# Four zero-filling stores of a gated attention and Mish mix, issued behind the gate's transfers in place of the opening

## The chip, the cores and the metric

The kernel runs on one core of a Trainium2 chip. The metric is the device time of one execution in microseconds (us). The core has a matrix engine (PE, whose weight loads are listed as PEld), a vector engine (DVE), a scalar engine (ACT), a general engine (POOL) and a sync engine (SP), which here does nothing but issue DMAs. Each engine works through its own list of instructions in order, and they wait for one another by semaphores.

## The reference

One input `x` of 2048 rows and 640 columns in bf16 goes through two branches, which a gate mixes row by row:

```python
g = sigmoid((x * gate_w).sum(-1, keepdims=True))
a = attention(x, wqkv) @ wo      # 32 heads of 20 columns, softmax over 2048 keys
h = x @ w1 + b1                  # 1536 columns
b = (h * tanh(softplus(h))) @ w2
out = g * a + (1 - g) * b
```

## The kernel before

**Tiling.** The rows are cut into four blocks of 512 queries (`QC`, `NQC = 4`), the 32 heads into eight head groups of four (`NQ = 8`). A head has 20 columns, and four heads lie in 32 partitions each, with 12 partitions of padding. A group `G` of the attention is one head group `p` with one block of queries `qc`; there are 32 of them. The first five head groups run one after the other through all four blocks (so groups 0 to 3 belong to head group 0, groups 4 to 7 to head group 1), the last three block by block.

**What a group does.** PE makes score tiles of 128 keys by 512 queries (line 1073), four heads at a time from four partition ranges. ACT takes the exponential of most of them (line 1091), and DVE and POOL work out the exponential of the others by integer arithmetic (lines 586 and 616). PE adds up the products with the values (line 1108). `normalise` divides by the sums and stores the result into `o_dram` (line 1184).

**Projections.** They run between the scores, in pieces of five matrix products (line 663). Queries and keys of head groups 1 to 7, and the queries of head group 0 from the second block on, take a way through HBM: DVE copies a product into a staging tile `st` (line 752; three tiles in turn), SP stores it into `q_dram` or `k_dram` (line 755), and later SP loads it into the padded tiles `qT` (`load_q`, line 780, four DMAs, one a head) or `kT` (`load_k`, line 772, four DMAs). The keys of head group 0 are made in place; their product `first_k_chain` also yields the 48 last key columns in the 12 padding partitions of each head, which `store_top` sends to `k_dram` (line 719, four DMAs of 12 partitions by 512 columns for each of the four blocks).

**The order of the work.** After the opening everything is issued in an order written out by hand (`ORDER`), one letter a step: `S` and `D` are score products, `x` an exponential on ACT, `F` a piece of a projection, `y` a waiting DVE operation, `q` and `k` the loads of queries and keys, `e` the three steps of the gate. A DVE operation can have a follow-up, such as a store, that is issued with it. SP's queue holds its DMAs in the order in which these steps call them.

**The opening.** It loads `x` and the first weights and transposes blocks 2 and 3 of `x` by DMA (line 472). Then it issues on SP the strips of weights `ws` (line 432), the value weights `wv` (line 1234, 800 KB), and the four stores that the change touches (lines 1245 to 1250). The first steps of `ORDER` follow: on SP's queue these are the four times four DMAs of line 719, two stores of line 755 into `q_dram` between and behind them, and the load of the queries of group 1 (step `q1`).

**The zeros.** In the last block of queries the two last head groups (`NSB = 2`) never go to `o_dram`: they stay on the chip in the tiles `O`, are multiplied by the gate's rows `g_rows`, and meet the zero-padded rows of `wo` (`wo_pad`) in the last products. Their 160 columns of these 512 rows in `o_dram` would be empty, but the transposing loads of line 923 read whole column blocks at the end of the kernel. So four stores of 128 rows by 160 columns (40 KB each) put zeros there. Their source is `wo_pad[7]`, which POOL has set to zero (line 1244) at 8 to 9 us, and into which line 1277 loads weights at 345 us and later.

**The gate.** Step `e0` (`gate_values`) is an exponential on ACT, `e1` loads `wo`, and `e2` (`gate_rest`) finishes the gate on DVE (lines 1256 to 1258), writes the last block's values into `g_dram` in four DMAs (line 1262), and reads them back into all partitions as `g_rows` in four more (line 1267). `g_rows` is read at line 1146, twice, from 657 us on. In `ORDER` the steps run `e0`, `e2`, and `e1` much later.

Of the kernel before, what the change touches and what calls it, by code (L numbers as in the profile page):

```python
# [9 lines left out]
P = 128  # L10
# [298 lines left out]
def kernel(  # L309
# [12 lines left out]
    nc = tc.nc  # L322
    _, S, D = A_x.shape
# [6 lines left out]
    QC = 512  # L330
    NQC = S // QC
    NU = QC // P
    NQ = H // 4
# [12 lines left out]
    NSB = 2  # L346
# [49 lines left out]
    wo_pad = {}  # L396
# [11 lines left out]
    o_dram = dram.tile([S, D], BF16, tag="o_dram", name="o_dram")  # L408
# [15 lines left out]
    HF = 4 * DH  # L424
# [78 lines left out]
    for n in (1, 2, 4, 8, 16):  # L503
        nc.vector.tensor_scalar(
            out=count[:, n : 2 * n], in0=count[:, 0:n], scalar1=float(n), scalar2=None, op0=ALU.add
        )
    nc.vector.transpose(out=count[:, 32:64], in_=count[:, 0:32])
    for k in range(0, P, 32):
        nc.vector.tensor_tensor(
            out=ident[k : k + 32, k : k + 32], in0=count[k : k + 32, 0:32],  # L510
# [405 lines left out]
    LQ = NQC - 1  # L916
# [297 lines left out]
    def first_product(bank, w, cols):  # L1214
# [14 lines left out]
        out=wv0[:, :, 4 * DH : 4 * DH + 1], in_=gate_w.rearrange("(kt p o) -> p kt o", p=P, o=1)  # L1229
# [8 lines left out]
        out=wkp[:, :, :, DH:32], in_=w_top[:, :, :].rearrange("p k (h d) -> p k h d", h=4)  # L1238
# [3 lines left out]
        wo_pad[p] = consts.tile([P, D], BF16, tag=tag, name=f"wo{p}")  # L1242
    for t_ in (*wo_pad.values(), *qTb[1 : NQT - 1], *T2, *kTb[1:]):
        nc.gpsimd.memset(t_, 0.0)
    for u in range(NU):
        r0 = LQ * QC + u * P
        nc.sync.dma_start(
            out=o_dram[r0 : r0 + P, (NQ - NSB) * HF : D],
            in_=wo_pad[NQ - 1][:, 0 : D - (NQ - NSB) * HF],
        )  # L1250

    def gate_values():
        nc.scalar.activation(g_t[:, :], z_t[:, :], ACT.Exp, scale=-1.0)
# [1 line left out]
    def gate_rest():  # L1255
        nc.vector.tensor_scalar(out=g_t, in0=g_t, scalar1=1.0, scalar2=None, op0=ALU.add)
        nc.vector.reciprocal(out=g_t, in_=g_t)
        nc.vector.tensor_scalar(
            out=g1_t, in0=g_t, scalar1=-1.0, scalar2=1.0, op0=ALU.mult, op1=ALU.add
        )  # L1260
        for r in range(4):
            nc.sync.dma_start(
                out=g_dram[:, :].rearrange("i (b r) -> i b r", r=4)[:, :, r],
                in_=g_t[32 * r : 32 * r + 32, NU * LQ : NU * LQ + NU],
            )
        for k in range(4):
            nc.sync.dma_start(out=g_rows[32 * k : 32 * k + 32, :], in_=g_dram[:, :])

    def load_wo():
        wo_sb[0] = work.tile([P, KT, D], BF16, tag="wvwo", name="wo_sb")  # L1270
        nc.sync.dma_start(
            out=wo_sb[0][:, :, :], in_=A_wo.rearrange("(kt p) c -> p kt c", p=P)
        )
        for p in wo_pad:
            for k in range(4):
                r0 = (4 * p + k) * DH
                nc.sync.dma_start(
                    out=wo_pad[p][32 * k : 32 * k + DH, :], in_=A_wo[r0 : r0 + DH, :]
                )
# [11 lines left out]
    def begin(k, bank):  # L1291
# [6 lines left out]
        "o": lambda qc, a, b: load_o(qc, range(a, b)),  # L1298
        "v": make_vd,
        "e": lambda i: (gate_values, load_wo, gate_rest)[i](),  # L1300
        "l": load_late,
        "d": d_take,
# [94 lines left out]
```

## Time and profile before

| | |
|---|---|
| median of 3 runs | 685.68 us (684.23 to 686.0) |
| the profiled execution, time | 685.34 us |
| its span, first to last instruction | 683.6 us |
| granted TensorE clock | 1.00 |
| the four stores issued | from 21.3 us, the last at 24.1 us |
| the gate's stores (line 1262) and loads (line 1267) issued | from 66.1 us, and from 72.2 to 74.1 us |
| first transposing load that reads `o_dram` | 480.5 us |

A row of the timeline or of the chain of waits has the start in us, the length in us, the engine, the line, the operation, the tiles it writes and reads, the count of instructions that are merged in it, and, where the engine was idle before it, for how long and what ended that. `SPq` stands for SP's sequencer, and its rows are the issues of DMAs: the length is the time that SP spends on issuing, not that of the transfer. In a row of the waits stand the total in us, the count, and the longest. In a row of windows stand the window, its length, the busy time and count of instructions of each engine, then the clock, the DMA engines' busy share and GB/s. In a row of one tile the three durations are the shortest, the median and the longest in ns.

### The profile page before, as it was taken

Reading aid. Unit: us, or ns where it says so; the run is one execution under the profiler, and the core shown is the slowest. Engines: PE = TensorE matmul, PEld = TensorE weight load, DVE = VectorE, ACT = ScalarE, POOL = GpSimd, SP = SyncE. Lnnn points to the kernel's source line nnn. Section 1 sums busy time; section 2 is a strip of 40 time slices with the busy share of each in tenths; the row PEclk is TensorE's granted clock in tenths of the full one; section 3 lists DMA queues with packets and bytes.
Section 4 is the critical chain, followed back from the end, with each engine's and each line's share of the span. In section 5 each row is a group of like instructions: output and inputs, shape, how many; then the busy total and the mean of one; then the engine's idle time right before and its main releaser. Section 6 shows DMA issues by size and latency. Waiting matters only on the chain.

```text
span 683.6 us, 24516 instructions
## 1 busy us (share of the span) xinstructions
PE 672.5 (98%) x10355; PEld 234.2 (34%) x10355; DVE 597.4 (87%) x1033; ACT 667.1 (98%) x692; POOL 354.0 (52%) x349
## 2 busy tenths in 40 slices
PE   8989999999999999999999999999999999999997
PEld 4433232323323443323333222222243333333334
DVE  5679989898989989898878988999999988799896
ACT  6999999999999999999999999999999999999996
POOL 5135555545463635565555654456546654555453
PEclk9999999999999999999999999999999999999999
DMA  8444321312311211111241223321232111141221
GB/s 170 106 88 148 64 50 38 67 40 55 95 27 37 61 46 36 26 35 32 37 104 33 41 55 72 66 51 38 56 94 57 21 48 30 41 66 35 59 86 59
DMA packets 128542, 40.47 MB, mean 59 GB/s; under 512 B 94960, under 2 KB 127872, under 8 KB 128432
## 3 DMA queue, kind: packets, MB, share of 16 engines
q1 hardware_dynamic: 126032, 38.29, 25.7%
q8 instruction: 81, 1.33, 0.9%
q10 hardware_dynamic: 2400, 0.62, 0.4%
q14 instruction: 29, 0.24, 0.1%
HBM read 22.29 MB, written 12.78 MB: 51 GB/s over the span
## 4 chain that ended last, share of the span: by engine, by line
PE 87%; ACT 8%; DVE 2%; issue 1%; DMA 1%; SPq 1%; POOL 0%; ACTq 0%; DVEq 0%
PE Sp L1073 29%; PE Sp L1108 29%; PE Sp L663 28%; ACT E L1091 6%; ACT big L871 2%; DVE T L586 1%; DMA wf<-in_A_wqkv_dram 1%; SPq L719 0%; PE Sp L1336 0%; DMA qT<-q_dram 0%; DVE T L1151 0%; DVE ot L1353 0%; PE Sp L1217 0%; PE Sp L1123 0%; ACT L1091 0%
## 5 line engine op out<-in xcount | busy, mean ns | idle before, releaser
L1091 ACT ACTIVATE E<-Sp 128x1024 bf16<-128x1024 f32 (+2 forms) x674 | 634.8, 1126 | 6.0 <-PE Sp L1073 5.1
L616 POOL INT64_ADD T<-T x334 | 344.1, 1042 | 315.9 <-DVE T L586 210.3
L586 DVE TENSOR_SCALAR T<-Sp 128x512 int16<-128x512 f32 x668 | 440.4, 683 | 57.7 <-PE Sp L1073 47.3
L1073 PE MATMUL Sp<-qT,kT 32*128 32x512 bf16 x2048 | 259.8, 384 | 4.6 <-DMA qT<-q_dram 1.8
L1073 PEld LDWEIGHTS <-kT 32*128 32x128 bf16 x2048 | 70.2, 91 | 246.5 <-issue 241.7
L1108 PE MATMUL Sp<-E,VA 128*21 128x512 bf16 x1380 | 128.0, 382 | 0.0
L1108 PE MATMUL Sp<-T,VD 128*21 128x512 bf16 x1288 | 117.9, 382 | 0.1
L663 PE MATMUL Sp<-w_sb,big 128*32 128x320 bf16 x1536 | 72.9, 302 | 0.2 <-DVE T L586 0.2
L663 PE MATMUL Sp<-xT,w1t 128*32 128x512 bf16 x960 | 72.2, 383 | 0.0
L1108 PEld LDWEIGHTS <-VA 128*21 128x21 bf16 x2048 | 44.0, 90 | 57.2 <-issue 48.4
L1108 PE MATMUL Sp<-T,VA 128*21 128x512 bf16 x668 | 63.5, 382 | 0.0
L663 PE MATMUL Sp<-xT,ws 128*32 128x512 bf16 x720 | 52.2, 382 | 0.0
L1108 PEld LDWEIGHTS <-VD 128*21 128x21 bf16 x1288 | 29.9, 90 | 38.6 <-issue 32.5
L663 PEld LDWEIGHTS <-big 128*32 128x32 bf16 x1536 | 33.0, 96 | 29.0 <-issue 21.8
L850 DVE TENSOR_SCALAR big<-Sp,b1f 128x512 bf16<-128x512 f32 x48 | 35.6, 742 | 1.8 <-PE Sp L663 1.2
L663 PE MATMUL Sp<-wv,xT 128*32 128x81 bf16 (+2 forms) x960 | 31.0, 257 | 0.0
L663 PEld LDWEIGHTS <-w1t 128*32 128x32 bf16 x960 | 19.8, 95 | 25.4 <-issue 17.4
L752 DVE CAST st<-Sp 128x512 bf16<-128x512 f32 x36 | 24.5, 681 | 2.7 <-PE Sp L663 2.4
L663 PE MATMUL Sp<-wo_sb,od 128*32 128x320 bf16 (+1 forms) x608 | 26.3, 301 | 0.1
L1137 DVE STREAM_TRANSPOSE T<-Sp 128x512 f32<-128x512 f32 x32 | 22.7, 709 | 2.6 <-PE Sp L1108 2.4
L663 PEld LDWEIGHTS <-xT 128*32 128x32 bf16 x960 | 18.8, 96 | 10.8 <-issue 7.7
L663 PEld LDWEIGHTS <-ws 128*32 128x32 bf16 x720 | 15.3, 95 | 19.5 <-issue 11.9
(76 smaller groups left out, 196.2 us busy)
## 6 DMA issues: line engine op xcount, KB each, us to landing
w1t<-in_B_w_dram SPq DMA_DIRECT2D x24, 320.0 KB
q_dram<-st SPq DMA_DIRECT2D x20, 128.0 KB
b_dram<-bt SPq DMA_DIRECT2D x16, 160.0 KB
bl<-b_dram SPq DMA_DIRECT2D x16, 160.0 KB
qT<-q_dram SPq DMA_DIRECT2D x124, 20.0 KB
o_dram<-T SPq DMA_DIRECT2D x120, 20.0 KB
out_dram<-ot SPq DMA_DIRECT2D x15, 160.0 KB
kT<-k_dram SPq DMA_DIRECT2D x28, 80.0 KB
```

Source lines behind the costliest of these rows:

```text
L586: nc.vector.tensor_scalar(out=dst.bitcast(I16), in0=src, scalar1=inv_sqrt_dh * LOG2E * 128.0, scalar2=127.0 * 128.0 + (BETA2 if two else B ...
L616: nc.gpsimd.int64_add(dst[:, :].bitcast(I64), src[:, :].bitcast(I64), n * 0x0001000100010001)
L663: nc.tensor.matmul(out_[k : k + 32], lhsT=lhsT[:, k : k + 32], rhs=rhs, tile_position=(0, k), **kw)
L752: nc.vector.tensor_copy(out=res["st"][:, :], in_=ps[:, :])
L850: nc.vector.tensor_scalar(out=big[:, pair_of(c, ft), (ft % 2) * QC : (ft % 2 + 1) * QC], in0=ps[:, :], scalar1=b1f[:, ft : ft + 1], scalar ...
L871: nc.scalar.activation(v, v, ACT.Mish)
L1073: nc.tensor.matmul(ps_cols, lhsT=kT[p][32 * t_ : 32 * t_ + 32, j * P : (j + 1) * P], rhs=qT[G][32 * t_ : 32 * t_ + 32, :], tile_position=( ...
L1091: nc.scalar.activation(E[:, x : x + n, :], allb[:, k0 : k0 + n, :], ACT.Exp, scale=inv_sqrt_dh,)
L1108: nc.tensor.matmul(acc[32 * t_ : 32 * t_ + DH + 1, :], lhsT=lhsT, rhs=rhs, start=(pv_done[G] == 0), stop=(pv_done[G] == pv_total[G] - 1), ...
L1137: nc.vector.transpose(out=st["T1"][:, :, :].rearrange("p b r -> p (b r)"), in_=acc[:, :])
```

## The change

The loop of the four stores leaves the opening and stands at the end of `gate_rest`, behind the loads of `g_rows`. Nothing else is touched: the same four DMAs, from the same tile to the same rows, on the same queue.

```diff
@@ -1242,12 +1242,6 @@
         wo_pad[p] = consts.tile([P, D], BF16, tag=tag, name=f"wo{p}")
     for t_ in (*wo_pad.values(), *qTb[1 : NQT - 1], *T2, *kTb[1:]):
         nc.gpsimd.memset(t_, 0.0)
-    for u in range(NU):
-        r0 = LQ * QC + u * P
-        nc.sync.dma_start(
-            out=o_dram[r0 : r0 + P, (NQ - NSB) * HF : D],
-            in_=wo_pad[NQ - 1][:, 0 : D - (NQ - NSB) * HF],
-        )
 
     def gate_values():
         nc.scalar.activation(g_t[:, :], z_t[:, :], ACT.Exp, scale=-1.0)
@@ -1265,6 +1259,12 @@
             )
         for k in range(4):
             nc.sync.dma_start(out=g_rows[32 * k : 32 * k + 32, :], in_=g_dram[:, :])
+        for u in range(NU):
+            r0 = LQ * QC + u * P
+            nc.sync.dma_start(
+                out=o_dram[r0 : r0 + P, (NQ - NSB) * HF : D],
+                in_=wo_pad[NQ - 1][:, 0 : D - (NQ - NSB) * HF],
+            )
 
     def load_wo():
         wo_sb[0] = work.tile([P, KT, D], BF16, tag="wvwo", name="wo_sb")
```

## The prediction

> **What bounds the kernel now.** I read the page first, then the windows of the first 60 us, then the chain of waits, then the order of issues on SP's queue.
>
> ```profile
> span 683.6 us, 24516 instructions
> PE 672.5 (98%) x10355; PEld 234.2 (34%) x10355; DVE 597.4 (87%) x1033; ACT 667.1 (98%) x692; POOL 354.0 (52%) x349
> 30.00:34.50 4.50, 4.50 (x125) 2.20 (x112) 4.12 (x13) 4.50 (x6) 2.05 (x2) 1.00 0.18 53
> 34.50:36.30 1.80, 0.03 (x6) 0.06 (x4) 0.35 (x2) 0.73 (x1) 0.00 (x0) 1.00 0.40 112
> 37.00:60.00 23.00, 23.00 (x407) 9.04 (x407) 18.86 (x35) 23.00 (x25) 10.55 (x11) 1.00 0.60 137
> 60.00:245.00 185.00, 184.76 (x2708) 60.90 (x2704) 168.44 (x285) 183.95 (x192) 92.73 (x91) 1.00 0.25 55
> ```
>
> The two lines of the page say that PE and ACT are both full. The window rows (length, then busy time of PE, PEld, DVE, ACT, POOL) show where they are not: from 34.5 to 36.3 us PE works for 0.03 us of 1.80. Before and after it PE has no gap. A microsecond won there stays won as long as ACT, just as full, gives way too.
>
> ```profile
> 34.20 0.29 SPq L780
> 34.54 1.60 DMA qT<-q_dram
> ...
> 34.12 0.39 PE L1108 MATMUL Sp<-T,VA 128*21 128x512 bf16 x4
> 36.27 0.40 PE L1073 MATMUL Sp<-qT,kT 32*128 32x512 bf16 x4 [1.77 <-DMA qT<-q_dram]
> 37.14 0.39 PE L1073 MATMUL Sp<-qT,kT 32*128 32x512 bf16 x3
> ...
> 36.82 1.45 ACT L1091 ACTIVATE E<-Sp 128x1536 bf16<-128x1536 f32 x1 [1.59 <-PE Sp L1073]
> ```
>
> The chain says who holds PE: the load of the second group's queries, whose second quarter is issued at 34.54 and lands at 36.14. PE is idle for 1.77 us from 34.51 on, and ACT for 1.59. So the question is why SP issues that load only at 34.20.
>
> ```profile
> 20.68 0.52 SPq L1234 DMA_DIRECT2D wv<-in_A_wqkv_dram  x1
> 21.32 3.20 SPq L1247 DMA_DIRECT2D o_dram<-wo  x4
> 24.61 1.33 SPq L719 DMA_DIRECT2D k_dram<-kT  x3
> 27.10 1.10 SPq L719 DMA_DIRECT2D k_dram<-kT  x3
> 30.74 0.35 SPq L755 DMA_DIRECT2D q_dram<-st  x1
> 31.98 1.67 SPq L719 DMA_DIRECT2D k_dram<-kT  x2
> 32.39 1.26 SPq L719 DMA_DIRECT2D k_dram<-kT  x1
> 33.74 0.34 SPq L755 DMA_DIRECT2D q_dram<-st  x1
> 34.20 1.41 SPq L780 DMA_DIRECT2D qT<-q_dram  x4
> 43.40 0.34 SPq L755 DMA_DIRECT2D k_dram<-st  x1
> ...
> SPq L719 <- DMA wv<-in_A_wqkv_dram: 1.1, 1, 1.1
> SPq L755 <- DVE st L752: 4.7, 1, 4.7
> ```
>
> SP is backlogged: it issues without a rest, some 0.4 us a DMA, until it waits for a producer again (4.7 us, ended at 43.40). One wait lies inside: 1.1 us for the landing of `wv`, ended at 27.10.
>
> **The change, part by part.** *Removed from the opening:* four issues. They hold SP from 21.32 until the first store of line 719 at 24.61, thus 3.29 us, and there is nothing else between.
>
> Not all of it reaches the query load. The scheduled program gives the DMAs eight completion semaphores in turn, and each DMA waits for the one eight places ahead. The eighth after `wv` now is the fourth store of line 719 (four `o_dram`, three `k_dram`, then the pause). With the four gone it is the eighth such store. `wv` itself is issued ahead of the edit, so I leave its landing at 27.1. What goes out ahead of that wait is then seven stores of line 719 in place of three, in the 5.8 us from 21.3 to 27.1: seven at 0.4 us are 2.8, so they fit even if two of them took 1.5 us each. Behind the wait there are four stores fewer ahead of the query load. From 27.10 to 30.74 nine stores go out, 0.404 us each; four are 1.62 us. The load's second quarter then is issued at 34.54 - 1.62 = 32.92 and, with the 1.60 us of its row, lands at 34.52. PE is free at 34.12 + 0.39 = 34.51.
>
> One term is left, the issue of 1.26 us at 32.39 where its neighbours take 0.36. Such a long one stands at 22.56 as well:
>
> ```profile
> L1247 SPq DMA_DIRECT2D o_dram<-wo x4: 432/578/1475, 21.3 to 24.1; - x4
> 22.56 1.48 SPq L1247 DMA_DIRECT2D o_dram<-wo  x1
> ```
>
> That both belong to a time and not to a kind of DMA is an estimate from these two rows. If the one at 32.39 stays at its clock time, it lies behind the first two quarters, which go out at about 31.65 and 32.0 (34.20 and 34.54 less 1.62 and less the 0.90 that it costs now). The second quarter lands at about 33.6, and the stall is gone. If it falls on that second quarter, this lands at 33.65 + 1.24 = 34.9 and 0.4 us of the stall stays. The bounds of this term are 1.77 and about 0.9 (it falls on the first quarter and the second waits behind). I take the full value, as SP's steps put the two issues ahead of 32.39, by little.
>
> The third and fourth quarter follow at 0.35 us each; the next products with these queries (37.14) come 0.87 us behind the first, so they hold nothing up. What the stores read is there in time:
>
> ```profile
> 23.08 0.69 DVE L709 CAST kT<-Sp 128x512 bf16<-128x512 f32 x1 [2.39 <-PE Sp L663]
> 29.17 0.69 DVE L752 CAST st<-Sp 128x512 bf16<-128x512 f32 x1
> ```
>
> The last copy into `kT` of the first head group ends at 23.77, and the last copy into a staging tile whose store stands ahead of the query load ends at 29.86; that store would be issued at about 31.2 (33.74 less 1.62 and 0.90). The load itself reads what the store of 30.74 writes and follows it by 3.46 - 0.90 = 2.56 us, against the 1.60 of a landing.
>
> How much of PE's 1.77 us becomes time: ACT has 25 instructions and no gap from 37 to 60 and gains 1.59 at its own stall (from 35.23). Where PE later waits for ACT (1.00 us at 246.75), ACT's gain counts, raised by gaps in which ACT waits for PE:
>
> ```profile
> ACT E L1091 <- PE Sp L1073: 0.5, 2, 0.3
> ...
> 246.75 0.40 PE L1073 MATMUL Sp<-qT,kT 32*128 32x512 bf16 x3 [1.00 <-ACT E L1091]
> ```
>
> That row, for 60 to 130 us, has 0.5 us of such gaps, so ACT can catch up the 0.18. Bounds 1.59 and 1.77; I take **1.70**, nearer to PE's.
>
> One rule counts against this size. The Trainium skill, "DMA: Bandwidth & Descriptors", section "Issuing engines are not separate DMA queues", says that the sequencer's time to initiate a DMA "is usually small relative to the DMA itself". By it the four stores' data would be what is saved: an estimate of 160 KB at the 143 GB/s that the trace moved from 20 to 30 us, 1.15 us, thus 684.2. The trace disagrees here: SP spends 3.20 us on issuing them.
>
> *Added behind the gate's transfers:* the same four issues, behind line 1267.
>
> ```profile
> 72.15 1.99 SPq L1267 DMA_DIRECT2D g_rows<-g_dram  x4
> 74.18 0.42 SPq L432 DMA_DIRECT2D ws<-in_A_wqkv_dram  x1
> 74.65 0.52 SPq L755 DMA_DIRECT2D q_dram<-st  x1
> 75.27 2.03 SPq L1184 DMA_DIRECT2D o_dram<-T  x4
> 83.75 1.39 SPq L772 DMA_DIRECT2D kT<-k_dram  x4
> ...
> SPq L1184 <- DVE T L1151: 1.2, 1, 1.2
> 83.66 0.68 DVE L752 CAST st<-Sp 128x512 bf16<-128x512 f32 x1
> 0.00:34.50 34.50, 8.77 (x62) 1.00 0.66 137
> 34.50:92.90 58.40, 22.32 (x179) 1.00 0.44 98
> 93.00 0.39 PE L1073 MATMUL Sp<-qT,kT 32*128 32x512 bf16 x3
> ```
>
> Everything from 74.18 on moves back by their issue time. Its bounds are 4 x 0.43 = 1.7 us (the shortest of the four) and 4 x 1.475 = 5.9 us (the longest); I take 3.2, what they take now. Two consumers come first. The copy of line 752 at 83.66 writes the staging tile that the store of 74.65 reads, three copies earlier. That store went out at 75.17; with the 1.60 us of the query load for its landing it is done at 76.8, so the cover is 6.9 us. The fifth group's keys and queries go out last at 83.75 + 1.39 = 85.14, landing at 86.7 by the same 1.60. They are first read at 93.00: the written order has 241 score products ahead of the first one of group 4, and the two rows above count 62 + 179 = 241 until 92.9. Cover 6.3 us. Behind that load SP waits 1.2 us for DVE ahead of line 1184's next stores, which takes that much of the delay back out. So 3.2 us, even 5.9, lie behind other work: **0**. Without that cover each microsecond would be one of PE. The last readers of the zeros and of `g_rows` come hundreds of microseconds later.
>
> *Sum.* The profiled execution took 685.34 us, 1.74 around its span of 683.6. 685.34 - 1.70 - 0 = **683.6**. It lies 0.34 under the median of the three runs, 685.68.
>
> **The rivals.**
>
> *A part of the stall stays.* The long issue falls on the query load itself, or `wv` lands later. For it: the two issues pass it by under 0.4 us. Against it: SP's steps. Gain 0.87 to 1.3: 684.0 to 684.5.
>
> *Nothing comes of it.* If `wv` or the tiles' copies set the pace rather than the issues, the load stays at 34.20: 685.3. Against it: behind 27.10 each issue follows the one before within 0.12 us, and the copies above end more than 1 us ahead of the new times of their stores.
>
> *Slower: the moved stores turn into a stall behind the gate.* Place: line 772's load of the keys ahead of 93.00. It decides from a delay of 6.3 us on, and the kernel is slower from 6.3 + 1.7 = 8.0 on. Price one for one: were each of the four to take double the longest one, 11.8 us, PE would stand for 5.5, and 685.34 - 1.70 + 5.5 = 689.1. For it: they would stand in line with line 1184's stores, whose issue is long too, and line 772 waits for a store queued behind them. Against it: no issue in these rows nears 2.95 us.
>
> **How the numbers follow.** A measurement of this kernel tells about 0.3% from no change, 2.06 us. The mark is 685.68 - 2.06 = 683.62, right at the forecast: with the whole 1.77 recovered it is 683.57, with ACT's 1.59 it is 683.75, and three runs of before spread over 1.77 us. I give the forecast 0.80, of it 0.50 below the mark and 0.30 above, since SP's steps give the whole stall and the median may fall like the profiled run. A part of the stall 0.09, nothing 0.03, slower 0.08. So faster 0.50, same 0.30 + 0.09 + 0.03 = 0.42, slower 0.08. The range goes from 683.57 less the runs' upper half-spread (1.45, from 685.68 down to 684.23) to the case in which nothing comes of it: 682.1 to 685.4. The slower case is left out.
>
> **What would show it.** In the changed profile: the first store of line 719 at about 21.3; the pause for `wv` behind the seventh of them and ended near 27.1; the query load issued at 31.6 to 32.6; no idle row of PE at line 1073 for it; ACT without the 1.59. Line 432's load about 3 us later against the gate's loads than now, and no new wait of PE or DVE from 74 to 100. The step on SP is wrong if `wv`'s wait stands elsewhere or ends later; the cover is wrong if PE waits for `kT` near 91. The prediction fails if PE's stall is gone and the span is still over 683, for then ACT, or something behind it, held the time.

## The result and the profile after

| | before | after |
|---|---|---|
| median | 685.24 us (21 runs, 684.06 to 687.32) | 684.40 us (21 runs, 683.58 to 685.33) |
| after to before, paired on each chip | | 0.9984, 95% interval 0.9977 to 0.9991 |
| the profiled execution, time and span | 685.34, 683.6 us | 683.58, 681.8 us |

The kernel is faster by 1.1 us (0.6 to 1.6), the ratio times 685.24; the medians differ by 0.84. The two profiled executions differ by 1.76, and that of after is the fastest of its 21. So the profiles show more than the runs, and most of the experiments below are about that difference.

The page of after and the windows that held the stall (length, then busy time of PE, PEld, DVE, ACT, POOL):

```profile
span 681.8 us, 24517 instructions
PE 672.8 (99%) x10355; PEld 234.2 (34%) x10355; DVE 597.3 (88%) x1033; ACT 666.7 (98%) x692; POOL 354.0 (52%) x349
30.00:34.50 4.50, 4.50 (x130) 2.26 (x116) 4.11 (x13) 4.50 (x6) 2.05 (x2) 1.00 0.31 98
34.50:36.30 1.80, 1.80 (x43) 0.81 (x43) 1.61 (x4) 1.80 (x2) 0.74 (x1) 1.00 0.50 117
```

From 34.5 to 36.3 PE works for all of the 1.80 us, where it had 0.03, and ACT too. The timeline of PE at that place has no idle time in brackets any more:

```profile
34.12 0.39 PE L1108 MATMUL Sp<-T,VA 128*21 128x512 bf16 x4
34.44 0.40 PE L1073 MATMUL Sp<-qT,kT 32*128 32x512 bf16 x4
```

The issues on SP's queue in the opening:

```profile
20.09 0.52 SPq L1234 DMA_DIRECT2D wv<-in_A_wqkv_dram  x1
20.73 7.49 SPq L719 DMA_DIRECT2D k_dram<-kT  x12
28.77 1.56 SPq L719 DMA_DIRECT2D k_dram<-kT  x4
30.43 0.35 SPq L755 DMA_DIRECT2D q_dram<-st  x1
30.89 1.41 SPq L780 DMA_DIRECT2D qT<-q_dram  x4
```

The long row of line 719 merges twelve issues. Two narrow windows of the same queue take it apart, from 23 to 24 and from 26 to 27 us:

```profile
22.81 1.59 SPq L719 DMA_DIRECT2D k_dram<-kT  x2
26.30 0.70 SPq L719 DMA_DIRECT2D k_dram<-kT  x2
```

And two of SP's waits (total, count, longest):

```profile
SPq L755 <- DVE st L752: 6.4, 1, 6.4
SPq L719 <- DMA wv<-in_A_wqkv_dram: 1.9, 1, 1.9
```

Seven stores of line 719 now go out ahead of the wait for `wv`, which has grown from 1.1 to 1.9 us; the eighth is issued at 26.30. From there to the query load are 30.89 - 26.30 = 4.59 us, against 34.20 - 27.10 = 7.10 before. The difference of 2.51 is the 1.62 of four stores and the 0.90 of the long issue, to a hundredth as forecast. (The long one falls on the seventh store, ahead of the wait: the pair from 22.81 takes 1.59.) The other 0.8 of the load's 3.3 us comes from `wv`, which landed earlier in this execution; 0.59 of it is its earlier issue (20.09 against 20.68). SP's following rest, waiting for DVE, has grown from 4.7 to 6.4.

Behind the gate's transfers, the timeline of SP's queue and the first product with the fifth group's keys:

```profile
70.61 2.01 SPq L1261 DMA_DIRECT2D g_rows<-g_dram  x4
72.67 1.85 SPq L1264 DMA_DIRECT2D o_dram<-wo  x4
74.61 0.39 SPq L432 DMA_DIRECT2D ws<-in_A_wqkv_dram  x1
82.78 1.39 SPq L772 DMA_DIRECT2D kT<-k_dram  x4
...
91.25 0.39 PE L1073 MATMUL Sp<-qT,kT 32*128 32x512 bf16 x3
```

The row of the four stores among those of the tensor `o_dram` (shortest, median and longest issue in ns):

```profile
L1264 SPq DMA_DIRECT2D o_dram<-wo x4: 424/432/436, 72.7 to 74.1; - x4
```

The four stores cost SP 1.85 us there, not 3.2: none of them is a long one. Line 432's load is issued 4.00 us behind the first of `g_rows`, against 2.03 before, so 1.97 later. The keys' load has gone out by 84.17, 7.1 us ahead of their first product, and PE has no wait for `kT` there.

### The profile page after: what moved, and what is told of

It reads as the page before. It is cut to its first block, busy times and chain, and to the rows that moved or that the text cites. A ratio compares the mean times of both kernels' runs of the same rounds, so it can differ in the third digit from the quotient of the medians.

```text
span 681.8 us, 24517 instructions
## 1 busy us (share of the span) xinstructions
PE 672.8 (99%) x10355; PEld 234.2 (34%) x10355; DVE 597.3 (88%) x1033; ACT 666.7 (98%) x692; POOL 354.0 (52%) x349
## 3 DMA queue, kind: packets, MB, share of 16 engines
q8 instruction: 81, 1.33, 0.9%
## 4 chain that ended last, share of the span: by engine, by line
PE 89%; ACT 7%; DVE 2%; issue 1%; POOL 0%; DVEq 0%; ACTq 0%
PE Sp L1108 30%; PE Sp L1073 30%; PE Sp L663 29%; ACT E L1091 5%; ACT big L871 2%; DVE T L586 0%; PE Sp L515 0%; PE Sp L1336 0%; DVE T L1151 0%; DVE ot L1353 0%; PE Sp L1217 0%; PE Sp L1123 0%; ACT L1091 0%; PE Sp L1199 0%; ACT big L966 0%
## 5 line engine op out<-in xcount | busy, mean ns | idle before, releaser
L1108 PEld LDWEIGHTS <-VD 128*21 128x21 bf16 x1288 | 29.8, 90 | 38.6 <-issue 32.6
```

The source lines that it names most:

```text
L1108: nc.tensor.matmul(acc[32 * t_ : 32 * t_ + DH + 1, :], lhsT=lhsT, rhs=rhs, start=(pv_done[G] == 0), stop=(pv_done[G] == pv_total[G] - 1), ...
```

## The experiments

**Theories** (1 to 3 in the texts that were written ahead of the runs). T1: PE's stall for the queries was all; its length varies between executions, and the new place is free. T2: the new place gives some 0.7 us back, which a still later one would gain. T3: the changed kernel keeps part of the stall in many executions. The profiled execution of after stands nearest to T1; the smaller median can be T2 or T3.

**The four stores in both places** (after, with the opening's loop put back):

```diff
     for t_ in (*wo_pad.values(), *qTb[1 : NQT - 1], *T2, *kTb[1:]):
         nc.gpsimd.memset(t_, 0.0)
+    for u in range(NU):
+        r0 = LQ * QC + u * P
+        nc.sync.dma_start(
...
```

> The stores stand in the opening and again behind the gate. Theory 1 (the stall before the second group's queries is all there is, its size varies from execution to execution with a mean near 1.1 us, and the place behind the gate costs nothing): ratio 1.000 to the kernel before, within 0.001, PE idle 0.8 to 2 us before 36.3. Theory 2 (the stall is worth 1.77 every time and the stores behind the gate give 0.7 of it back): 1.001, about 0.7 us slower. Theory 3 (the place costs nothing, but the changed kernel keeps a part of the stall in many executions): 1.000.

684.67 us (12 runs) against 684.84 for before (35 runs beside this and the next three kernels): ratio 1.0001 (0.9987 to 1.0015). PE's and SP's timeline:

```profile
26.94 0.40 PE L663 MATMUL Sp<-xT,ws 128*32 128x512 bf16 x4 [0.77 <-issue]
...
31.71 1.41 SPq L780 DMA_DIRECT2D qT<-q_dram  x4
73.39 1.85 SPq L1270 DMA_DIRECT2D o_dram<-wo  x4
```

The stores behind the gate cost SP the same 1.85 us. The ratio is that of T1 and T3, but its interval does not exclude T2's 1.001. With the opening of before, however, the query load went out at 31.71 and PE did not wait for it at all: in this execution `wv` was issued at 19.32 and no issue behind it was a long one. It waited somewhere else: 0.77 us ahead of a piece of a projection, for nothing that the profile names ("issue"). No theory had that.

**The four stores in neither place** (issued at the head of step `e1`, ahead of `wo`):

```diff
         for k in range(4):
             nc.sync.dma_start(out=g_rows[32 * k : 32 * k + 32, :], in_=g_dram[:, :])
-        for u in range(NU):
...
     def load_wo():
+        for u in range(NU):
...
```

> The stores go neither into the opening nor behind the gate but ahead of the loads of wo, some 270 us later. Theory 1: the changed kernel's ratio, 0.998 to 0.999. Theory 2: 0.997 to 0.9975, the whole 1.77. Theory 3: 0.998 to 0.999.

684.23 us (11 runs), ratio 0.9991 (0.9981 to 1.0001). In the timeline PE waits as in the kernel above, for less:

```profile
26.66 0.40 PE L663 MATMUL Sp<-xT,ws 128*32 128x512 bf16 x4 [0.44 <-issue]
```

The row of the four issues, far behind everything that waits for SP:

```profile
L1266 SPq DMA_DIRECT2D o_dram<-wo x4: 432/440/1853, 343.5 to 346.4; - x4
```

It gains no more than after does, and the 0.997 to 0.9975 of T2 lies outside the interval, so nothing speaks for T2. The unnamed wait stands here too.

**Line 719's sixteen stores out of the opening** (into the second step `l`), once on after and once on before:

```diff
+    tops = []
+
     def load_late(i):
         if i < 2:
             load_strip(i, 1, nc.sync)
+            if i == 1:
+                for c in tops:
+                    store_top(c)
...
-            return [(lambda x=x: copy(*x)) for x in parts], lambda: store_top(c)
+            return [(lambda x=x: copy(*x)) for x in parts], lambda: tops.append(c)
```

> The changed kernel, and the sixteen stores of line 719 are issued behind the strips of the step l1, where SP waits over 6 us for DVE. The load of the second group's queries then has nothing of the wv wait ahead of it. Theory 1: as the changed kernel, 0.998 to 0.999, since no stall is left there. Theory 2: the same. Theory 3: 0.997 to 0.9975, since what is left of the stall goes too.

> The kernel before, its four stores in the opening, with the sixteen stores of line 719 deferred in the same way. Theory 1: 0.998 to 0.999, the stall gone by another way. Theory 2: 0.997 to 0.9975, the stall gone and nothing paid behind the gate. Theory 3: 0.997 to 0.9975.

On after 684.41 us, 0.9996 (0.9986 to 1.0006); on before 684.03, 0.9998 (0.9986 to 1.0009), 12 runs each. In the profile of the second, with the four zero stores still in the opening, the query load goes out early and PE waits for nothing:

```profile
28.21 1.44 SPq L785 DMA_DIRECT2D qT<-q_dram  x4
```

So, as far as one profile shows, it was the count of issues ahead of that load on SP that made the stall, not these four stores as such. On after, PE has the unnamed wait again, 0.87 us. The 0.997 to 0.9975 that T3 expected of both kernels (T2 of the second) lies outside both intervals, and of T1's 0.998 to 0.999 only the upper end lies inside. That the ratios hardly leave 1 although no wait for queries is left in these profiles says that something else costs time in many executions; the intervals, 0.2 to 0.3% wide, are too wide to say more.

**The same kernels again**, with no edit: other profiled executions of before and of after.

> The kernel before, unchanged, one more profiled execution. Theory 1 in the form that the runs so far suggest (two kinds of opening: A, in which the fifth DMA transpose of the second five takes 2.7 us on SP and wv is issued at 20.1 us or later; B, in which it takes 1.3 and wv is issued before 19.8): in A PE waits 1.2 to 1.9 us for the queries at 34.5 and not at 26; in B PE waits 0.4 to 0.9 us at 26.2 for no producer, and under 0.2 at 34.5. Against it (the stall at 34.5 is there each time): over 1 us at 34.5 whatever the opening.

> The kernel before once more, expected as before_2; over the looks at the kernel before, theory 1 wants opening A in about half to two thirds of them, since the change is worth about 1.1 us of the 1.77.

> The kernel before a third time, expected as before_2 and before_3: over 1 us idle at 34.5 where wv is issued at 20.1 us or later, and none where it is issued before 19.8.

> The changed kernel, one more profiled execution. Theory 1: no wait for the queries at 34.5 in either opening; in A none at 26 either and a span near 681.8, in B 0.4 to 0.9 us at 26.2 and a span near 682.5. Against it (theory 3, a part of the stall stays): an idle row for the queries at 34.5.

686.69, 687.05 and 686.74 us for before, 684.73 for after, and 685.79 in the one run of before beside them. All four expectations missed. The three executions of before, with `wv` issued at 20.6 to 20.9, were to wait at 34.5 and not at 26; they have the unnamed wait at 26, of 1.80, 2.09 and 1.81 us, and only 0.83 to 0.89 of the wait for the queries. after_2 was to have no wait for the queries and has 1.13. The timeline of the first of them, SP's queue and PE:

```profile
18.76 1.80 SPq L432 DMA_DIRECT2D ws<-in_A_wqkv_dram  x1
20.61 0.53 SPq L1234 DMA_DIRECT2D wv<-in_A_wqkv_dram  x1
...
25.88 0.61 PE L663 MATMUL Sp<-xT,ws 128*32 128x512 bf16 x8
28.30 0.40 PE L663 MATMUL Sp<-xT,ws 128*32 128x512 bf16 x4 [1.80 <-issue]
...
37.63 0.40 PE L1073 MATMUL Sp<-qT,kT 32*128 32x512 bf16 x4 [0.83 <-ACT E L1091]
```

The last row names ACT, whose exponential ended at 37.53; but the second quarter of the load of the queries landed at 37.50, and in the profile of after the same product starts at 34.44, while ACT's exponential at that place still runs until 35.24. So it is the load that PE needed, as the same row of before_4 says:

```profile
37.68 0.40 PE L1073 MATMUL Sp<-qT,kT 32*128 32x512 bf16 x4 [0.88 <-DMA qT<-q_dram]
```

In each of the three a long issue, of 1.44 to 1.48 us, falls on the first or second quarter of that load.

The DMA queues of before_2 (packets, MB, share of the 16 engines), the first row for 24 to 26 us, the other two for 26 to 27:

```profile
q1 hardware_dynamic: 974, 0.63, 98.3%
...
q8 instruction: 1, 0.02, 6.0%
q1 hardware_dynamic: 6, 0.00, 1.2%
```

A queue that the trace calls "instruction" moves one packet, and it does so only when the data queue, 98% busy until then with `wv` and the four stores behind it, has run empty. The list of DMA queues on the page of after tells whose it is:

```profile
q8 instruction: 81, 1.33, 0.9%
```

81 packets in the execution of after, 1.33 MB, thus 16.4 KB each; PE has 2 x 10355 = 20710 instructions, 255.7 a packet. From this I read q8 as PE's program. The Trainium skill, "Runtime: NRT & Kernel Launch", section "Instruction fetch mechanics", says that an engine fetches its instructions over a DMA queue of its own, in blocks of 16 KiB or 256 instructions; the trace agrees. The Trainium skill calls the cost "mostly hidden" there; here the fetch took up to 2.37 us of PE.

*Theory F.* PE's third fetch falls due near `wv`'s 800 KB. If it gets in ahead of that data or among it, it costs PE nothing; if it queues behind, PE runs out of instructions. Narrow windows give the packet's start, and the table sets it beside PE's two waits, for every profiled execution, those of the experiments further below among them:

| execution | third fetch starts | unnamed wait, and its end | wait for the queries | PE's last end | less the two waits |
|---|---|---|---|---|---|
| before | 22.71 | 0 | 1.77 | 679.79 | 678.02 |
| before_2 | 26.00 | 1.80, 28.30 | 0.83 | 681.15 | 678.52 |
| before_3 | 26.40 | 2.09, 28.58 | 0.89 | 681.50 | 678.52 |
| before_4 | 26.00 | 1.81, 28.28 | 0.88 | 681.19 | 678.50 |
| before_5 | 25.89 | 2.37, 28.32 | 0 | 683.06 | 680.69 |
| both | 24.58 | 0.77, 26.94 | 0 | 678.93 | 678.16 |
| top_before | 21.45 | 0 | 0 | 677.93 | 677.93 |
| after | 23.08 | 0 | 0 | 678.05 | 678.05 |
| after_2 | 21.64 | 0 | 1.13 | 679.09 | 677.96 |
| after_3 | 24.36 | 0.66, 26.68 | 0 | 678.71 | 678.05 |
| late | 24.32 | 0.44, 26.66 | 0 | 678.68 | 678.24 |
| top_after | 24.68 | 0.87, 26.95 | 0 | 678.94 | 678.07 |
| split_only | 23.46 | 0 | 0.41 | 678.49 | 678.08 |
| split | 23.09 | 0 | 0 | 678.72 | 678.72 |

The unnamed wait stands where the fetch starts at 24.3 or later, in all eight, and ends 2.2 to 2.4 us behind that start; where it starts by 23.46 there is none. Less both waits, PE ends at 677.9 to 678.5 in all but two: before_5 (below) and split, which has another gap, 0.88 us at 9.15. The two waits in the opening are what tells these executions apart, to 0.6 us.

The DMA packets of the traces bear the theory out. `wv` moves as 640 packets of 1280 bytes. In the eight executions with the unnamed wait all of them start ahead of the third fetch (in `late` 616); in before, top_before, after and after_2, which have `wv` in one piece and no such wait, 605, 640, 400 and 640 start behind it.

In before, a late fetch takes PE to the queries later, so the wait for them shrinks from 1.77 to under 0.9: the first loss hides part of the second. And after_2 shows T3 at work. In its timeline, SP's queue and PE, and in its chain of waits, the second quarter of the load:

```profile
31.74 2.45 SPq L780 DMA_DIRECT2D qT<-q_dram  x4
...
35.58 0.40 PE L1073 MATMUL Sp<-qT,kT 32*128 32x512 bf16 x4 [1.13 <-DMA qT<-q_dram]
...
32.08 3.36 DMA qT<-q_dram
```

The instruction queue from 32.6 to 33.9 us:

```profile
q8 instruction: 1, 0.02, 5.7%
```

The query load left 2.46 us earlier than in the first profile of before, and its second quarter went out at 32.08; but that quarter landed 3.36 us later, in place of 1.60, and 1.13 us of the stall stayed. A fetch started at 32.62, in between. The four issues took 2.45 us in place of 1.41 because the last of them was a long one, which PE did not wait for. That the fetch held the landing up is argued from the times alone.

**Room for the fetch.** If theory F holds, `wv` in pieces lets the fetch pass between them. On after, two of its five pieces stay in the opening and one goes behind each of the first three steps of `first_k_chain`:

```diff
+    def load_wv(a, b):
+        for kt in range(a, b):
+            nc.sync.dma_start(out=wv[:, kt, :], in_=wrows[:, kt, 2 * D : 3 * D])
...
+            def done():
+                store_top(c)
+                if c < 3:
+                    load_wv(2 + c, 3 + c)
...
-    nc.sync.dma_start(out=wv[:, :, :], in_=wrows[:, :, 2 * D : 3 * D])
+    load_wv(0, 2)
```

> The changed kernel with wv in five pieces, the pieces three to five behind the stores of line 719 of the first three blocks, and those stores where they were. Theory F: no wait over 0.3 us at 26; the query load goes out at about 32, so a fetch near 32 us can still hold it up, by 0 to 1.2 us at 34.5. Ratio 0.9975 to 0.9985. Against it: a wait of 0.4 to 2 us at 26.

In `split`, the stores of line 719 for blocks 2 and 3 also wait for the second step `l`:

```diff
             if i == 1:
+                store_top(2)
+                store_top(3)
...
             def done():
-                store_top(c)
+                if c < 2:
+                    store_top(c)
```

> The changed kernel; wv is loaded in five pieces (two in the opening, one behind each of three steps between the stores of line 719), and the stores of line 719 for the last two blocks go behind the strips of the step l1. Theory F (both stalls of the opening come from PE's instruction fetches: one that starts late, behind the 800 KB of wv, makes PE wait at 26 us by about its start less 23.9; one near 32 us holds up the query load): the fetch of 22 to 24 us is never behind more than 320 KB, so no wait over 0.3 us at 26; the query load goes out at about 30.3 and lands ahead of 32.3, so none at 34.5; PE's last instruction ends at 678.0 to 678.5, span near 681.9, ratio to the kernel before 0.997 to 0.998. Against it (the fetch is late for a reason of its own): a wait of 0.4 to 2 us at 26 stays and the ratio is that of the changed kernel, 0.998 to 0.9995.

Beside them, after and before once more, with no edit:

> The changed kernel, another profiled execution. Theory F: its time is PE's end at 678.0 to 678.5 plus the waits at 26 (0, or 0.4 to 2 us where the third fetch starts later than 24) and at 34.5 (0, or about 1.1 us where the fetch near 32 us meets the query load); nothing else between 20 and 100 us. Against it: a wait of PE or DVE between 70 and 100 us, or a sum that does not fit by more than 0.5 us.

> The kernel before, another profiled execution on the same chip. Theory F: PE's end is 678.0 to 678.5 plus its waits at 26 and at 34.5 to 37, together 0.8 to 3 us, and the wait for the queries is there (0.8 to 1.8 us) unless SP's issues behind wv ran without a long one. Against it: a sum that does not fit by more than 0.5 us.

| | median | range | ratio to before (685.31, 23 runs) |
|---|---|---|---|
| split_only, 12 runs | 684.06 us | 683.56 to 684.99 | 0.9979 (0.9968 to 0.9991) |
| split, 11 runs | 683.76 us | 683.42 to 684.22 | 0.9973 (0.9964 to 0.9982) |

The fetch starts at 23.46 and 23.09, and the unnamed wait is gone from both. Ahead of it stand 253 and 256 packets of `wv`; the two pieces of the opening are 256. Nor had these two executions drawn the lucky opening: their second fetch starts at 18.80 and 19.52 us, and in all seven executions with `wv` in one piece where it starts at 18.0 or later the unnamed wait follows. It is one profile of each kernel.

What is left in split_only is 0.41 us for the queries. It is the late landing of after_2 again: the second quarter, issued at 31.38, landed 3.44 us later, with a fetch at 32.59 in between. In split, with eight issues fewer ahead of it, the load went out 0.49 us earlier, its fetch came at 32.95, and PE did not wait. First split_only's PE and that quarter in its chain, then split's PE and SP:

```profile
34.96 0.40 PE L1082 MATMUL Sp<-qT,kT 32*128 32x512 bf16 x4 [0.41 <-DMA qT<-q_dram]
...
31.38 3.44 DMA qT<-q_dram
```

```profile
26.08 0.83 PE L670 MATMUL Sp<-xT,ws 128*32 128x512 bf16 x12
...
30.55 1.41 SPq L793 DMA_DIRECT2D qT<-q_dram  x4
...
35.16 0.40 PE L1086 MATMUL Sp<-qT,kT 32*128 32x512 bf16 x4
```

Split's runs spread over 0.80 us, after's over 1.75 and before's over 3.26 (in other runs): as both waits go, the executions grow alike. Split is 1.85 us faster than before by the paired ratio (1.2 to 2.5; medians 683.76 against 685.31); with after it was not timed side by side.

The execution of after, 684.37 us, had the late fetch, with a wait of 0.66, and its sum fits theory F. That of before, 688.71, does not fit: PE's end less its waits is 680.69, where 678.0 to 678.5 was expected, and no wait for the queries is left. It had the longest unnamed wait of all, and clock rows that the others have not. Its windows from 26 to 38 us (the third number from the end is the clock):

```profile
26.00:28.30 2.30, 0.00 (x0) 0.00 (x0) 0.17 (x1) 0.96 (x1) 0.00 (x0) 0.95 0.08 15
28.30:31.00 2.70, 2.68 (x22) 0.53 (x26) 1.29 (x2) 1.02 (x1) 0.00 (x0) 0.50 0.10 24
31.00:34.00 3.00, 3.00 (x39) 0.91 (x39) 0.73 (x2) 2.54 (x3) 0.00 (x0) 0.50 0.21 64
34.00:38.00 4.00, 4.00 (x120) 1.77 (x108) 3.34 (x9) 2.84 (x4) 2.05 (x2) 0.89 0.38 106
```

After 2.37 us of idleness PE works at half the clock for at least 5.7 us. The 680.69 is 2.2 us later than in the other three executions of before with the late fetch. The half clock is the likely cause; nothing else was tried for it.

The timed runs, which carry their mean clock, show that this is not a single case. Of the 58 runs of before that were timed beside the experiments six have 0.997, and of the 47 of both, late, top_after and top_before six have 0.997 or 0.998; all twelve took 686.3 us or more. Of the 44 of after, split_only and split none is under 0.999. So some of the slowest executions lost clock as well; that the change prevents this is not shown, as `late`, with the same opening as after, has one such run in 11.

## Why the prediction was right or wrong

*What bounds the kernel.* Right for the profiled execution: the load of the queries held PE, and with it gone PE and ACT run through. For the kernel it was only half of it. In four of five profiled executions of before, PE loses 1.80 to 2.37 us at 26 us to its own program, and at most 0.89 to the queries.

*Removed: SP's steps.* Right where they were worked out: seven stores ahead of the wait for `wv`, four issues fewer behind it (1.62 us), no long one ahead of the load (0.90), 2.51 in all. The 0.90 was luck: the long issue was to stay at its clock time, 32.39, but no issue near it was long in this execution, and in before_2 to before_4 one fell on the load itself. The load went out at 30.89, ahead of the forecast 31.6 to 32.6, by the 0.8 us that `wv` landed earlier; I had left that landing at 27.1.

*ACT's part.* The 1.70 chosen between 1.59 and 1.77 is 1.76 in the one pair of profiles that has the stall in full before and not after; ACT did not hold it back.

*The rule weighed.* By the Trainium skill's remark that initiation is usually small ("DMA: Bandwidth & Descriptors", "Issuing engines are not separate DMA queues") the time would be 684.2, and 684.40 lies near it. The trace does not bear out the reason: deferring other issues did away with the stall with the zeros still in the opening (top_before), and the four stores hold SP for 1.85 us behind the gate, in after and in both. Their data do count, at a place that the rule doesn't speak of (below).

*Added behind the gate.* Right at 0. The delay was 1.97 us, near the lower bound and not the 3.2 chosen, as the long issue did not move with the stores; no wait followed it, and the later place gained nothing. The slower rival falls with it.

*The sum, and its term that was off.* "685.34 - 1.70 - 0 = 683.6", and "the median may fall like the profiled run". A gain of 1.1 us (0.6 to 1.6) was measured, 0.16%, so under the 0.3% that the prediction set as its mark and gave 0.50. The median of 684.40 lies in the band of the rival "a part of the stall stays" (684.0 to 684.5), which had 0.09. That the profiled execution of after took 683.58, as forecast, is chance: it is the fastest of 21. The mechanism was right for the opening that it was read from, and the term of the stall was mis-sized: 1.77 is what it was in one execution. Over the six profiled openings with the four stores in (before, before_2 to before_5, both) it is 0.73 on the mean, and over the four without (after, after_2, after_3, late) 0.28, so 0.45 of difference. The rival "a part of the stall stays" is one of those four, after_2, though not by the mechanism that it named: the long issue fell on the last quarter of the load, and it was the landing of the second that came late. A long issue on the load itself stood in three profiles of before.

*What the prediction did not have.* The change also shortens the other wait: on the mean 1.47 us with the stores in the opening, 0.28 without. Part of that is chance, as an early fetch or a late one is decided ahead of the edit. But among the late ones the fetch starts 5.26 to 5.51 us behind the issue of `wv` with the stores there (both, before_2 to before_5), and 4.58 to 4.99 without (late, after_3, top_after). The two groups do not overlap. Half a microsecond is what 160 KB take at the 320 to 360 GB/s of that stretch. The zeros move as 512 packets of 320 bytes, and in those five late openings with the stores 462 to 488 of them start ahead of the fetch; in before and top_before, with the early fetch, none does. So the zeros' data stand ahead of the fetch; that the half microsecond is theirs was not tried alone. The two differences, 0.45 and 1.19, come to 1.6 us, the upper end of what was measured; ten executions on several chips don't give it closer.

*What stays open.* How often each opening comes. The second fetch seems to decide it. Among the twelve executions with `wv` in one piece it starts at 17.3 us in three, and all three have the early third fetch; at 17.6 in two, one of each kind; at 18.0 to 19.0 in seven, and all seven have the late one. The code up to there is the same in both kernels, and what moves the second fetch was not found.

## What to carry to other kernels

A stall of a microsecond or two in one profile is one draw: profile the unchanged kernel several times before a term of the sum is taken from it, above all in the opening, where a wait at one place eats the wait at the next. Follow a load to its landing as well as to its issue: in two executions it went out in time and landed late. A queue that issues without a rest up to a load that someone waits for is worth emptying, and issues that nobody awaits cost nothing where the next consumer has some microseconds of cover. When an engine waits for nothing that the profile names, set its instruction queue beside the big loads: an 800 KB load in one piece can keep it without a program.

## What the runs showed of the hardware

- **A program fetch queues behind data.** In the eight late openings the third block of PE's instructions came only behind the data of `wv` (640 of its 640 packets, in `late` 616); PE stood for 0.44 to 2.37 us and went on 2.2 to 2.4 us after the fetch's start. In pieces, `wv` let it pass behind 253 and 256 packets.
- **Long issues on SP come with fetches.** Both long issues of before (22.56 and 32.39), the seventh store of after (23.2) and the last quarter of the query load of after_2 (32.83) each stand by a fetch (22.71, 32.12, 23.08, 32.62). Not every fetch makes one: that of after at 32.34 has issues of the usual 0.35 us beside it. A cause was not tested.
- **A load can land late beside a fetch.** The second quarter of the query load landed 3.36 us after its issue in after_2 and 3.44 in split_only, with a fetch at 32.62 and 32.59 in between, against 1.60 in before. A fetch in between does not always do it: after and both have one (32.34, 33.22) and landings of 1.5 us. A cause was not tested.
- **The clock's drop.** Idle for 2.37 us, PE was granted half its clock for 5.7 us or more; idle for 1.77 to 2.09 us it kept 1.00, which the windows of before from 37 us on, that of before_2 from 28.30 and this one of before_3, with the 2.09, show:

```profile
28.50:31.00 2.50, 2.42 (x29) 0.66 (x29) 1.29 (x2) 1.54 (x2) 0.00 (x0) 1.00 0.11 26
```

The Trainium skill, "TensorE: Matmul & The Clock Gate", "Part 1: The HAM clock gate", puts the drop behind an idle window of about 3.4 us, free-running. Here less idleness than that was enough once, at 2.37 us.
